# Fused squared-ReLU attention and GELU feed-forward: full-width k transfers, a list-scheduled opening, and the first k by a hardware queue

## The chip, the cores and the metric

The kernel runs on one core of one Trainium2 chip. The metric is device time in microseconds (us) of one execution, and quoted times are medians of several executions. Each execution also has a span, from its first to its last instruction, and a mean granted TensorE clock. The profile is of one execution, so a span can lie a few us off the median time.

Engines are named as in the profile: PE is the matmul engine (TensorE), ACT is ScalarE, DVE is VectorE, POOL is GpSimd, SP is SyncE. SP computes nothing here: it only issues transfers.

## The reference, cut to what matters

```python
# q, k, v: (8 batches, 12 heads, 448 rows, 64)   float32
scores = q @ k.T / sqrt(64)
attn   = maximum(scores, 0) ** 2 / 448
x      = (attn @ v), heads side by side          # (8*448, 768)
out    = gelu(x @ w_in) @ w_out                  # 768 -> 2048 -> 768, float32
```

## The kernel before

Work goes batch by batch, and the parts of a batch are called as follows in this text:

- **Transposes.** q and k are brought into transposed form. Batches 0 to 2 do it on PE, batches 3 to 7 with transfers that transpose, issued by SP ("DMA transposes").
- **Attention.** A quad is four heads. A step is a QK product (L172), a relu on ACT (L180), a square on DVE (L182) and an AV product (L192). DVE then moves the result to `xT`.
- **ffn1** multiplies by `w_in` (L211), and ACT's gelu writes `h_sb`. **ffn2** multiplies by `w_out` (L227); DVE copies the result in two halves into an output tile `osb` (L235), and SP stores the tile.

In the loop over batches, the attention of batch b is woven with ffn1 of b-1 and ffn2 of b-2, so that PE always has something to do.

```python
    opool = pool("opool", 2)          # two output tiles
    f_pp = pool("f_pp", 2, PS)        # two PSUM tiles for ffn1, ffn2 and PE transposes
    ...                               # (cut)
    ROWS = ((KC,) * 4, (128, 128, 128, 64))   # rows of a transpose: q, k
    ...
    def transpose_dma(b):
        for w in (1, 0):
            off = 0
            for t, r in enumerate(ROWS[w]):
                nc.sync.dma_start_transpose(
                    get_T(b)[w][:, :, off : off + r], perm[b][w][:r, t, :]
                )
                off += r
    ...
    def ffn2(pr, t, n):
        if n == 0:
            osbs[pr, t] = opool.tile([128, DM], F32, tag="osb", name="osb")
        ...                           # 16 matmuls into po
        nc.vector.tensor_copy(osb[:, bass.ts(n, ND)], po[:, :ND])
        if n == 1:
            ...
                nc.sync.dma_start(rows[c, p0 : p0 + m, :], osb[j - 128 * t : j - 128 * t + m, :])
    ...
    for b in range(2, B):
        ...
        l = 10 if b == 2 else 2
        prep[l] = nxt                 # permute_k, permute_q, transpose_dma of batch b+1
        ...
        weave(todo, atoms, prep)      # emits work in program order, on all engines
```

Of the kernel before, what the change touches and what calls it, by code (L numbers as in the profile page):

```python
# [8 lines left out]
F32 = mybir.dt.float32  # L9
# [5 lines left out]
NC = S // KC  # L15
KB = 64
NK = S // KB
HP = H // 2
# [9 lines left out]
def kcol(i):  # L28

    return i * 128 if i < 4 else (i - 4) * 128 + 64  # L30
# [3 lines left out]
def kernel(  # L34
# [22 lines left out]
    permpool = pool("perm", 1)  # L57
# [12 lines left out]
    q32 = const.tile([KC, 4, NC * D], F32, tag="q32", name="q32")  # L70

    def load(b, g0, g1):
        h0, h1 = 4 * g0, 4 * g1
        if b not in nq:
            nq[b] = natpool.tile([KC, H, NC * D], BF16, tag="nq", name="nq")
            nk[b] = natpool.tile([128, H, 4 * D], BF16, tag="nk", name="nk")
            vt[b] = vpool.tile([128, G, 2, NK * D], BF16, tag="v", name="v_sb")
        kk = k[b, h0:h1].rearrange("h (p i) d -> p h (i d)", i=NK)
        nc.gpsimd.dma_start(nk[b][:KB, h0:h1, :], kk[:, :, : 4 * D])  # L79
        nc.gpsimd.dma_start(nk[b][KB:, h0:h1, : 3 * D], kk[:, :, 4 * D :])  # L80
        qq = q[b, h0:h1].rearrange("h (p c) d -> p h (c d)", c=NC)
        if b > 0 or g0 > 0:
            nc.gpsimd.dma_start(nq[b][:, h0:h1, :], qq)  # L83
        else:
            nc.sync.dma_start(q32, qq)
        vv = v[b].rearrange("(g j e) (p i) d -> g j p e (i d)", j=2, e=2, i=NK)
        for g in range(g0, g1):
            for j in range(2):
                nc.gpsimd.dma_start(vt[b][64 * j : 64 * j + 64, g], vv[g, j])  # L89
# [4 lines left out]
    def load_win(i):  # L94
        w = moe_w_in.rearrange("(kd p) f -> p kd f", p=128)
        nc.gpsimd.dma_start(win_sb[:, :, bass.ts(i, FF // 4)], w[:, :, bass.ts(i, FF // 4)])
# [6 lines left out]
    qkT, perm = {}, {}  # L103

    def get_T(b):
        if b not in qkT:
            qkT[b] = (
                tpool.tile([128, HP, S], BF16, tag="qT", name="qT"),
                tpool.tile([128, HP, S], BF16, tag="kT", name="kT"),
            )  # L110
        return qkT[b]

    def get_perm(b):
        if b not in perm:
            perm[b] = (
                permpool.tile([KC, NC, DM], BF16, tag="pq", name="pq"),
                permpool.tile([128, 4, DM], BF16, tag="pk", name="pk"),
            )
        return perm[b]


    def permute_q(b, g0=0, g1=G):
        h = slice(4 * g0, 4 * g1)
        pq = get_perm(b)[0].rearrange("p c (h d) -> p h c d", d=D)
        sq = nq[b].rearrange("p h (c d) -> p h c d", d=D)
        nc.vector.tensor_copy(pq[:, h], sq[:, h])  # L126

    def permute_k(b, g0=0, g1=G):
        h = slice(4 * g0, 4 * g1)
        pk = get_perm(b)[1].rearrange("p c (h d) -> p h c d", d=D)  # L130
        sk = nk[b].rearrange("p h (c d) -> p h c d", d=D)
        nc.vector.tensor_copy(pk[:, h, :3], sk[:, h, :3])  # L132
        nc.vector.tensor_copy(pk[:KB, h, 3], sk[:KB, h, 3])  # L133

    ident = const.tile([128, 128], BF16, tag="ident", name="ident")
    ROWS = ((KC,) * 4, (128, 128, 128, 64))

    def transpose_pe(b, g, w, copy):

        tp = f_pp.tile([128, 2, S], BF16, tag="f", name="tp")  # L140
        for j in range(2):
            off = 0
            for t, r in enumerate(ROWS[w]):
                nc.tensor.transpose(  # L144
                    tp[:, j, off : off + r],
                    perm[b][w][:r, t, bass.ts(2 * g + j, 128)],
                    ident[:r, :r],
                )
                off += r
        copy(get_T(b)[w][:, 2 * g : 2 * g + 2, :], tp)  # L150

    def transpose_dma(b):
        for w in (1, 0):
            off = 0
            for t, r in enumerate(ROWS[w]):
                nc.sync.dma_start_transpose(
                    get_T(b)[w][:, :, off : off + r], perm[b][w][:r, t, :]
                )
                off += r
# [4 lines left out]
    xT, hT, asq, pav = {}, {}, {}, {}  # L164

    def qk_step(b, g, i):
        qT, kT = get_T(b)
        ps = s_pp.tile([128, 2, NB], F32, tag="s", name="ps")
        for e in range(2):
            r = slice(64 * e, 64 * e + 64)  # L170
            for j in range(2):
                nc.tensor.matmul(  # L172
                    ps[64 * j : 64 * j + 64, e, :S],
                    kT[r, 2 * g + j, kcol(i) : kcol(i) + KB],
                    qT[r, 2 * g + j, :],
                    start=True,
                    stop=True,
                )
        ar = apool.tile([128, 2, S], BF16, tag="ar", name="a_relu")
        nc.scalar.activation(ar, ps[:, :, :S], AF.Relu, scale=c_att)  # L180
        a2 = apool.tile([128, 2, S], BF16, tag="a2", name="a_sq", bufs=8)
        nc.vector.tensor_mul(a2, ar, ar)  # L182
        asq[b, g, i] = a2

    def av_step(b, g, i):
        if i == 0:
            pav[b, g] = [av_pp.tile([128, NB], F32, tag="av", name="pav") for j in range(2)]
        a2 = asq.pop((b, g, i))
        for j in range(2):
            r = slice(64 * j, 64 * j + 64)  # L190
            for e in range(2):
                nc.tensor.matmul(  # L192
                    pav[b, g][j][64 * e : 64 * e + 64, :S],
                    vt[b][r, g, e, bass.ts(i, D)],
                    a2[r, e, :],
                    start=(i == 0),
                    stop=(i == NK - 1),
                )
        if i == NK - 1:
            if b not in xT:  # L200
                xT[b] = xpool.tile([128, HP, S], BF16, tag="xT", name="xT")
            for j in range(2):
                nc.vector.tensor_copy(xT[b][:, 2 * g + j, :], pav[b, g][j][:, :S])  # L203


    def ffn1(b, m):
        if b // 2 not in hT:
            hT[b // 2] = hpool.tile([128, KF, 2 * S], BF16, tag="h", name="h_sb")
        ph = f_pp.tile([128, NB], F32, tag="f", name="psh")
        for kd in range(KD):  # L210
            nc.tensor.matmul(  # L211
                ph[:, :S],
                win_sb[:, kd, bass.ts(m, 128)],
                xT[b][:, kd, :],
                start=(kd == 0),
                stop=(kd == KD - 1),
            )
        nc.scalar.activation(hT[b // 2][:, m, (b % 2) * S : (b % 2 + 1) * S], ph[:, :S], AF.Gelu)  # L218
# [3 lines left out]
    def ffn2(pr, t, n):  # L222
        if n == 0:
            osbs[pr, t] = opool.tile([128, DM], F32, tag="osb", name="osb")
        po = f_pp.tile([128, NB], F32, tag="f", name="pso")
        for kf in range(KF):
            nc.tensor.matmul(  # L227
                po[:, :ND],
                hT[pr][:, kf, bass.ts(t, 128)],
                wout_sb[:, kf, bass.ts(n, ND)],  # L230
                start=(kf == 0),
                stop=(kf == KF - 1),
            )
        osb = osbs[pr, t]
        nc.vector.tensor_copy(osb[:, bass.ts(n, ND)], po[:, :ND])  # L235
        if n == 1:
            j = 128 * t
            while j < 128 * t + 128:
# [6 lines left out]
                nc.sync.dma_start(rows[c, p0 : p0 + m, :], osb[j - 128 * t : j - 128 * t + m, :])  # L245
                j += m

    def f1(b):
        return [(1.14, ffn1, (b, m)) for m in range(KF)]

    def f2(b):
        tiles = range(0, 3) if b % 2 == 0 else range(3, 7)
        return [(2.6, ffn2, (b // 2, t, n)) for t in tiles for n in range(2)]
# [16 lines left out]
    def run_av(keep):  # L270

        while len(lag) > keep:
            st = lag.pop(0)
            av_step(*st)
            if st[2] == NK - 1:
                break

    def qk(sts):
        for st in sts:
            qk_step(*st)  # L280
            lag.append(st)

    def run(atoms):
        for c, fn, a in atoms:
            fn(*a)

    def steps(b):
        return [(b, g, i) for g in range(G) for i in range(NK)]

    def weave(todo, atoms, prep):  # L290
# [4 lines left out]
        for l in range(0, n, 2):  # L295
            for p in prep.get(l, ()):
                p()
            run_av(0)
            qk(todo[l : l + 2])
            while atoms and done < total * (l + 2) / n - 0.01:  # L300
                done += atoms[0][0]
                run([atoms.pop(0)])
        run(atoms)
# [146 lines left out]
```

## Time and profile before

| | before |
|---|---|
| time, median | 424.91 us (423.57 to 426.17) |
| span of the profiled run | 421.0 us |
| PE busy | 395.6 us, 94% |
| ACT busy | 213.3 us, 51% |
| DVE busy | 186.1 us, 44% |
| POOL busy | 60.9 us, 14% |

PE bounds this kernel: some 25 us of the span are all that it leaves free, of which some 18 lie in the first 75 us. The prediction below shows the views that say so. The chain of work that ended last, as shares of the span by engine ("q" behind an engine's name means its transfer queue):

```profile
PE 87%; DVE 5%; ACT 4%; issue 2%; DMA 1%; POOL 0%; ACTq 0%; DVEq 0%; POOLq 0%
```

### The profile page before, as it was taken

To read this page: it belongs to the slowest core of one execution; us is meant where nothing else is said; L and a number is where in the kernel's file an instruction comes from. 1 tells how busy PE (TensorE), PEld (TensorE's weight loads), DVE (VectorE), ACT (ScalarE), POOL (GpSimd) and SP (SyncE) were. 2 spreads that over 40 slices of the span, in tenths; PEclk is the share of its full clock that TensorE was granted. 3 is DMA by queue.
4 is the path that set the end of the run, shared out by engine and by line. 5 is a ranking of instruction groups with operands and counts; after the bars stand their busy time and mean duration, and the time that the engine had idled before them with its cause. 6 is when DMAs were issued, how large, how long until landed. Compare 5 with 4: busy or idle time off the path is not lost.

```text
span 421.0 us, 7489 instructions
## 1 busy us (share of the span) xinstructions
PE 395.6 (94%) x3152; PEld 200.8 (48%) x3152; DVE 186.1 (44%) x330; ACT 213.3 (51%) x302; POOL 60.9 (14%) x94
## 2 busy tenths in 40 slices
PE   2958998999989999999999999999999999999995
PEld 1323444554545545545445455545455455555562
DVE  1776656336446444464455443463453543300121
ACT  4875665654553556456564565465564654223200
POOL 8363060404104100050005000000000000000000
PEclk9998999999999999999999999999999999999998
DMA  9999399974995990199516990162011111001122
GB/s 141 159 156 200 63 164 209 205 117 78 174 191 85 172 173 15 39 140 166 99 37 92 179 174 2 39 142 66 2 37 39 39 37 29 24 26 37 39 75 75
DMA packets 68417, 41.41 MB, mean 98 GB/s; under 512 B 36640, under 2 KB 64800, under 8 KB 68384
## 3 DMA queue, kind: packets, MB, share of 16 engines
q0 software_dynamic: 35280, 22.58, 38.7%
q1 hardware_dynamic: 33104, 18.36, 22.3%
q8 instruction: 24, 0.39, 0.4%
q14 instruction: 9, 0.07, 0.1%
HBM read 45.61 MB, written 11.01 MB: 135 GB/s over the span
## 4 chain that ended last, share of the span: by engine, by line
PE 87%; DVE 5%; ACT 4%; issue 2%; DMA 1%; POOL 0%; ACTq 0%; DVEq 0%; POOLq 0%
PE pso L227 35%; PE psh L211 34%; PE pav L192 9%; PE ps L172 7%; ACT a_relu L180 4%; PE tp L144 2%; DVE a_sq L182 2%; DMA nk<-in_k_dram 1%; DVE xT L203 1%; DVE qT L150 1%; DVE kT L150 0%; DVE pk L132 0%; DVE pq L126 0%; POOL nk L79 0%; DVE osb L235 0%
## 5 line engine op out<-in xcount | busy, mean ns | idle before, releaser
L180 ACT ACTIVATE a_relu<-ps 128x896 bf16<-128x896 f32 x168 | 144.7, 916 | 116.6 <-PE ps L172 116.6
L211 PE MATMUL psh<-xT,win_sb 128*128 128x448 bf16 x768 | 156.6, 353 | 0.0
L227 PE MATMUL pso<-wout_sb,h_sb 128*128 128x384 bf16 x896 | 152.8, 326 | 0.0
L182 DVE TENSOR_TENSOR a_sq<-a_relu 128x896 bf16<-128x896 bf16 x168 | 104.4, 624 | 91.0 <-ACT a_relu L180 90.6
L227 PEld LDWEIGHTS <-h_sb 128*128 128x128 bf16 x896 | 86.3, 98 | 63.1 <-issue 5.9
L211 PEld LDWEIGHTS <-win_sb 128*128 128x128 bf16 x768 | 70.5, 98 | 79.4 <-issue 19.7
L218 ACT ACTIVATE h_sb<-psh 128x448 bf16<-128x448 f32 x128 | 70.0, 547 | 60.9 <-PE psh L211 60.9
L235 DVE COPY osb<-pso 128x384 f32<-128x384 f32 x56 | 31.2, 558 | 110.3 <-PE pso L227 110.3
L192 PE MATMUL pav<-a_sq,v_sb 64*64 64x448 bf16 x672 | 53.8, 370 | 10.0 <-DVE a_sq L182 5.2
L172 PE MATMUL ps<-qT,kT 64*64 64x448 bf16 x672 | 51.9, 368 | 4.1 <-ACT a_relu L180 2.8
L203 DVE CAST xT<-pav 128x448 bf16<-128x448 f32 x48 | 27.7, 619 | 16.2 <-PE pav L192 16.2
L192 PEld LDWEIGHTS <-v_sb 64*64 64x64 bf16 x672 | 16.3, 107 | 38.7 <-issue 36.9
L79 POOL DMA_DIRECT2D nk<-in_k_dram x12 | 9.4, 783 | 149.8 <-DVE pk L133 139.3
L89 POOL DMA_DIRECT2D v_sb<-in_v_dram x48 | 29.0, 628 | 14.3 <-DMA nk<-in_k_dram 8.9
L172 PEld LDWEIGHTS <-kT 64*64 64x64 bf16 x672 | 21.2, 108 | 20.6 <-issue 9.3
L144 PE MATMUL tp<-ident,pq 112*128 112x112 bf16 x72 | 6.2, 241 | 5.6 <-ACT pq L329 5.6
L83 POOL DMA_DIRECT2D nq<-in_q_dram x11 | 9.5, 859 | 0.7 <-DMA nk<-in_k_dram 0.5
L132 DVE COPY pk<-nk 128x768 bf16<-128x768 bf16 (+1 forms) x14 | 7.1, 510 | 5.4 <-DMA nk<-in_k_dram 5.4
L144 PE MATMUL tp<-ident,pk 128*128 128x128 bf16 x72 | 8.6, 232 | 0.4 <-DVE pk L132 0.4
L80 POOL DMA_DIRECT2D nk<-in_k_dram x12 | 8.4, 703 | 3.5 <-DMA win_sb<-in_moe_w_in_dram 3.5
L144 PEld LDWEIGHTS <-pk 128*128 128x128 bf16 x72 | 5.5, 101 | 5.5 <-DVE a_sq L182 1.2
L144 PEld LDWEIGHTS <-pq 112*128 112x128 bf16 x72 | 4.5, 112 | 7.4 <-ACT pq L329 5.6
(18 smaller groups left out, 32.8 us busy)
## 6 DMA issues: line engine op xcount, KB each, us to landing
v_sb<-in_v_dram POOLq DMA_DIRECT2D x48, 112.0 KB, 13.6
nq<-in_q_dram POOLq DMA_DIRECT2D x6, 672.0 KB, 14.8
win_sb<-in_moe_w_in_dram POOLq DMA_DIRECT2D x4, 768.0 KB, 10.2
wout_sb<-in_moe_w_out_dram POOLq DMA_DIRECT2D x2, 1536.0 KB, 16.9
out_dram<-osb SPq DMA_DIRECT2D x8, 336.0 KB, 2.8
nk<-in_k_dram POOLq DMA_DIRECT2D x6, 384.0 KB, 7.1
out_dram<-osb SPq DMA_DIRECT2D x8, 288.0 KB, 2.6
out_dram<-osb SPq DMA_DIRECT2D x8, 240.0 KB, 2.8
```

What stands on the lines that cost most here:

```text
L83: nc.gpsimd.dma_start(nq[b][:, h0:h1, :], qq)
L89: nc.gpsimd.dma_start(vt[b][64 * j : 64 * j + 64, g], vv[g, j])
L144: nc.tensor.transpose(tp[:, j, off : off + r], perm[b][w][:r, t, bass.ts(2 * g + j, 128)], ident[:r, :r],)
L172: nc.tensor.matmul(ps[64 * j : 64 * j + 64, e, :S], kT[r, 2 * g + j, kcol(i) : kcol(i) + KB], qT[r, 2 * g + j, :], start=True, stop=True,)
L180: nc.scalar.activation(ar, ps[:, :, :S], AF.Relu, scale=c_att)
L182: nc.vector.tensor_mul(a2, ar, ar)
L192: nc.tensor.matmul(pav[b, g][j][64 * e : 64 * e + 64, :S], vt[b][r, g, e, bass.ts(i, D)], a2[r, e, :], start=(i == 0), stop=(i == NK - 1),)
L203: nc.vector.tensor_copy(xT[b][:, 2 * g + j, :], pav[b, g][j][:, :S])
L211: nc.tensor.matmul(ph[:, :S], win_sb[:, kd, bass.ts(m, 128)], xT[b][:, kd, :], start=(kd == 0), stop=(kd == KD - 1),)
L218: nc.scalar.activation(hT[b // 2][:, m, (b % 2) * S : (b % 2 + 1) * S], ph[:, :S], AF.Gelu)
L227: nc.tensor.matmul(po[:, :ND], hT[pr][:, kf, bass.ts(t, 128)], wout_sb[:, kf, bass.ts(n, ND)], start=(kf == 0), stop=(kf == KF - 1),)
L235: nc.vector.tensor_copy(osb[:, bass.ts(n, ND)], po[:, :ND])
```

## The change

Its intent is to shorten the opening, the first 75 us:

1. **Quads regrouped.** k and v are laid out so that one transfer fills 128 partitions. `w_in`'s rows are permuted to match, which takes three transfers per quarter in place of one. A k quad then is seven 128x128 blocks in place of rows of 128, 128, 128 and 64.
2. **A list-scheduled opening.** Operations carry dependencies, buffers and assumed durations. A scheduler picks, at each moment, the one that can start first. Batch 0's attention runs by half sequences, so that ffn1 of batch 0's first half can start early.
3. **First k by a hardware queue** (ACT's), in float32, for POOL's queue. The first q comes by SP's queue in float32, as before, but only half of it comes first.

From batch 2 on, PE's order is given to the scheduler as a fixed list, and so are those of POOL and SP. The core of the diff, much cut:

```diff
+class Scheduler:
+    ...
+    def run(self, fixed):             # fixed: engine -> list whose order is kept
+    ...
-        kk = k[b, h0:h1].rearrange("h (p i) d -> p h (i d)", i=NK)
-        nc.gpsimd.dma_start(nk[b][:KB, h0:h1, :], kk[:, :, : 4 * D])
-        nc.gpsimd.dma_start(nk[b][KB:, h0:h1, : 3 * D], kk[:, :, 4 * D :])
+            nc.gpsimd.dma_start(nk[b][:, 2 * g0 : 2 * g1], kv_view(k, b, g0, g1))
 ...
+    nc.scalar.dma_start(k32, kv_view(k, 0, 0, 1))
+    nc.sync.dma_start(q32, q_view(0, 0, 1, 0, HC))
 ...
+    def add_T_dma(b):
+        for g in range(G):
+            ...
+            op = sch.add((("SP", 0.9, 12.0),), fn, [Pk[b, g]] + old_T(b))
+            sp_q.append(op)
+        for c in range(NC):
+            ...
+            op = sch.add((("SP", 0.9, 12.0),), fn, [Pq[b, g, c] for g in range(G)] + old_T(b))
+            sp_q.append(op)
 ...
+        if n == 1:                    # in add_f2
+            st = sch.add((("SP", 0.3, 2.5),), store, [ev], frees=("osb",))
+            sp_q.append(st)
 ...
     for b in range(2, B):
+        add_steps(steps(b))
+        if b + 1 < B:
+            ...
+            add_T_dma(b + 1)          # appends seven transposes to sp_q
+        ...
         x1, x2 = f1(b - 1), f2(b - 2) # f2 appends its stores to sp_q, after them
 ...
+    sch.run({"PE": pe_q, "POOL": pool_q, "SP": sp_q})
```

## The prediction

> **What bounds the kernel now.** I read the windows view first, cut where the stages change: the first QK matmul starts at 8.93 us, batch 0's last relu ends at about 35.9, and batch 2's interleaved stretch begins with the QK at 75.22. Columns: window, its length, then busy us (instructions) of PE, PEld, DVE, ACT, POOL, then granted clock, DMA share, GB/s.
>
> ```profile
> 0.00:8.93 8.93, 2.19 (x16) 1.37 (x16) 1.43 (x5) 3.44 (x4) 7.83 (x17) 1.00 0.90 140
> 8.93:35.90 26.97, 20.10 (x208) 8.50 (x211) 18.48 (x38) 19.48 (x23) 13.83 (x22) 0.95 1.15 164
> 35.90:75.22 39.32, 34.69 (x329) 16.71 (x324) 25.09 (x51) 25.38 (x36) 10.79 (x15) 0.99 1.01 157
> 75.22:421.00 345.78, 338.66 (x2609) 174.23 (x2608) 141.07 (x237) 165.05 (x239) 28.46 (x43) 1.00 0.52 86
> ```
>
> From 75.22 on PE is busy 98% with ACT and DVE below half: that part is bound by PE's own matmuls, and the part of the 7 us not busy is mostly the last store. The first 75 us hold about 18 us of idle PE. The waits view, for PE before 75.22 and then after it, says on what:
>
> ```profile
> PE tp L144 <- ACT pq L329: 5.6, 1, 5.6
> PE pav L192 <- DVE a_sq L182: 3.3, 5, 2.1
> PE pav L192 <- DVE xT L203: 3.0, 5, 1.7
> PE ps L172 <- ACT a_relu L180: 2.8, 9, 0.6
> PE pav L192 <- DMA win_sb<-in_moe_w_in_dram: 1.8, 1, 1.8
> ```
> ```profile
> PE pav L192 <- DVE a_sq L182: 1.9, 5, 0.4
> ```
>
> So the opening is a chain of first load, cast, transposes, then relu, square and eviction, with PE issuing in a hand-written order. The timeline of ACT shows how fast batch 0's attention can go and how it is broken:
>
> ```profile
> 24.71 5.78 ACT L180 ACTIVATE a_relu<-ps 128x896 bf16<-128x896 f32 x7 [1.57 <-PE ps L172]
> 33.19 0.92 ACT L180 ACTIVATE a_relu<-ps 128x896 bf16<-128x896 f32 x1 [2.70 <-PE ps L172]
> 34.90 0.92 ACT L180 ACTIVATE a_relu<-ps 128x896 bf16<-128x896 f32 x1 [0.79 <-PE ps L172]
> ```
>
> Seven relus in 5.78 us is one per 0.81-0.83 us; 21 of them need 17.2 us, and batch 0 took 27. Between the groups ACT waits for PE, which waits for an eviction or a transpose queued behind something else. The page's slice rows say that DMA is saturated in most of the first 40 us and that the clock drops once:
>
> ```profile
> PEclk9998999999999999999999999999999999999998
> DMA  9999399974995990199516990162011111001122
> ```
>
> **What the Trainium skill says.** "DMA: Bandwidth & Descriptors", Rules for kernel authors, advises one 128-partition transfer instead of two to disjoint halves, and its section SWDGE vs HWDGE vs iDMA says that a cast during the transfer needs the GpSimd queue. The trace agrees with the second as far as it goes: the one load on SP (q) lands in float32 and is cast by ACT in 1.045 us. "TensorE: Matmul & The Clock Gate", Part 1, says PE starts at half clock and falls back after about 3.4 us of idleness. Agreed: four QK matmuls show 0.59 us up to 18 us and 0.38 after, and 0.59 again near 34-36 after the idle stretch at 29-32. "TensorEngine Tiling (Array Packing)", Key Properties, says that a change of tiling mode drains PE. Agreed: 12 ffn1 matmuls after attention take 2.38 us, 18 with none before 3.40, so a switch costs 2.38 - 12 x 0.189 = 0.11 us. "ScalarE: Activation LUTs", What ACT_TABLE_LOAD costs, gives 186 ns + 0.833 N, with 93 ns of overlap back to back: 932 for N = 896, the trace has 916; 559 for 448, the trace has 547. From it I estimate 0.28-0.37 us for the new 224-column activations.
>
> **The change part by part.** Everything from batch 2 on keeps its PE order, as the comparison of instruction orders shows (same runs of QK, AV, ffn1, ffn2). So the span is 345.8 us plus the moment at which batch 2's stretch starts (75.2 now), and what that moment gains comes off the measured 424.9.
>
> (1) First loads. k comes by ACT's queue, half of q by SP's: 0.46 + 0.23 MB of float32. Now 0.46 MB of q lands at 4.5 and k through POOL at 6.3. At the 380 GB/s which the DMA rows show around 2.5-3.5 us, 0.69 MB takes 1.8 us; begun at 1.8 and with about 0.8 to completion, both are there at 4.4. The casts (ACT 512 elements, about 1.1 us in two pieces; DVE 896 float32 elements, about 1.0) end at 5.5. Half of q means four transposes for eight. The cold transposes and kT's copy (0.62) put the first QK at 7.7 for 8.93: -1.2 us.
>
> (2) K transposes. Rows of 128, 128, 128, 64 become seven full 128x128 per quad. Now they cost
>
> ```profile
> 54.37 0.87 PE L144 MATMUL tp<-ident,pk 128*128 128x128 bf16 x8
> 55.17 0.57 PE L144 MATMUL tp<-ident,pq 112*128 112x112 bf16 x8
> 55.67 0.57 PE L192 MATMUL pav<-a_sq,v_sb 64*64 64x448 bf16 x8
> ```
>
> 0.80 us from start to start for k, 0.50 for q of equal count: the two 64-row ones change the tiling mode and cost the extra 0.3-0.4. Ten quads up to 75 us, two later: -4 us of PE work, -0.8 of it certain (batch 2's last two quads); the rest counts only where PE is the bound.
>
> (3) Batch 0's attention by half sequences, in pairs: 20 full relus and 2 half ones for 21. ACT: 20 x 0.81 + 2 x 0.45 = 17.1, two qT copies of 448 (0.9), four xT copies of 224 (1.2): 19.2 us. First relu about 8.3, so 27.5, plus some 2 us of stalls while PE is cold (cold QK and AV pairs are 0.37 each, 0.75 of each 0.81 slot, and two quads of transposes do not fit beside them): 29.5 for 35.9.
>
> (4) Batch 1 with ffn1 of batch 0 in halves. ACT: 21 x 0.81 = 17.0, 17 half gelus by 0.35 = 6.0, copies 2.4: 25.4, giving 55 for the last relu. Then square and AV, about 1.2, of which part is covered, 66 half ffn1 matmuls at an estimated 0.10 (6.6), transposes and their two copies (2.2): batch 2's stretch begins at about 65.
>
> (5) PE as a check. Transposes 10 x (0.39 + 0.39 + 0.2 for switches) = 9.8; batch 0's 84 half steps at 0.11 = 9.2 (0.095 by columns, more for four weight loads, which take 0.11-0.13); batch 1's 42 steps at 0.19 = 8.0; 32 half ffn1 at 0.60 = 19.2; about 40 further switches by 0.1 = 4; cold clock about 5; start 5.5: 60.7 us. PE and ACT are thus both close to full, and neither order can be perfect: I put 65.5, so -9.7, and -0.8 from (2): 424.9 - 10.5 = 414.4.
>
> (6) Loads. Batch 0, batch 1 and w_in are the same 14.5 MB of float32 as now; the k pieces of 512 and 384 bytes become 896, w_in's grow in number from 4 issues to 12. At 340-400 GB/s (170-200 of the bf16 that the DMA rows count) all are in by 40-43 us; batch 1's third quad is wanted at about 45. Batch 2 and w_out follow without the present gap at 45-52 us.
>
> **Rivals.** (a) DMA stays the bound: the DMA row is at 9 for most of the first 40 us and nothing fewer is loaded. Against: much of that is the loader running ahead, and only 1.8 us of PE's waits name a DMA. If it holds, batch 1's last quad slips by 3-4 us and the time is 418. (b) PE becomes the bound in the opening: twice the number of attention matmuls and ffn1 matmuls with the same weight loads for half the columns, more switches, a cold clock. For: my sum has only 5 us to spare. If a half step costs 0.19 as the full one does, 84 x 0.08 = 6.7 us more: 419-421. (c) The static order, fixed from assumed durations on all engines, is wrong where the chip differs, and the strict order on ACT and DVE turns a late load into waits after 75 us too, where now there are 2: +2-4 us. (d) Better than thought: the denser opening warms the clock at about 14 us for 19 and keeps it (now 3.4 us are lost half again at 33-36), and ACT runs unbroken: batch 2 begins at 61, time 410.
>
> **Range and chances.** The PE sum makes about 409.5 the floor; (a) or (b) alone give 418-421. So 410 to 420 for eight in ten. The 2% line is 416.4, inside the range and above the centre by 2: faster 0.62, same 0.35, slower 0.03 (only if (b) and (c) add up).
>
> **What would show it.** In the new profile: first QK at 7.7 +- 0.5; batch 0's relus ending at 28-31; batch 2's first QK pair at 63-68 and from there to the end 345 +- 1.5; PE idle before that at 9-12 us for 18, of which about 5 at the start; k transposes at 0.4 per quad; no clock drop at 33-36. Wrong if the tail after batch 2's start grows, if PE's waits name k, q or w_in loads for over 2 us, or if half steps take near 0.19.

## More of the kernel before

`weave` emits everything in program order: an engine gets its instructions in the order in which the code reaches them. `transpose_dma(b+1)` stands inside the weave, after the first steps of batch b, and so it comes into SP's queue between the stores of output tiles.

SP's timeline in batch 2's stretch; columns: start, duration in us, queue, line, kind of transfer, destination<-source, number.

```profile
97.31 0.81 SPq L245 DMA_DIRECT2D out_dram<-osb  x2
100.39 6.04 SPq L156 DMA_TRANSPOSE kT<-pk  x4
106.48 12.85 SPq L156 DMA_TRANSPOSE qT<-pq  x4
119.43 12.35 SPq L245 DMA_DIRECT2D out_dram<-osb  x6
```

SP issues the first finished tile (two stores, since its rows lie in two strips of the output), and only then the eight DMA transposes. These occupy it for 6.04 + 12.85 = 18.9 us. Then come the stores of the next tiles.

## The result, and the profile after

| | before | changed |
|---|---|---|
| time, median | 424.58 us (423.57 to 426.17) | 440.41 us (439.93 to 440.92) |
| span of the profiled run | 421.0 us | 438.2 us |
| start of batch 2's stretch | 75.22 us | 64.16 us |
| from there to the end | 345.78 us | 374.04 us |
| PE busy | 395.6 us, 94% | 397.0 us, 91% |

The changed kernel is slower: the ratio is 1.037 (95% interval 1.033 to 1.041). Ratios here are the mean time of one kernel's fast runs over that of the other's of the same rounds, so not quite the ratio of the medians quoted. (The before column has one more run than the section above.)

The windows view of the changed kernel, cut as in the prediction: first QK, near the end of batch 0's last relu (which ends at 30.66, a little before the cut), batch 2's stretch. Columns as there.

```profile
0.00:8.17 8.17, 1.30 (x13) 1.04 (x13) 1.82 (x6) 2.20 (x4) 7.04 (x14) 1.00 0.84 170
8.17:32.00 23.83, 21.50 (x430) 15.66 (x431) 20.79 (x53) 21.80 (x35) 13.66 (x21) 1.00 1.33 199
32.00:64.16 32.16, 29.65 (x362) 21.34 (x362) 20.46 (x45) 26.74 (x51) 7.46 (x9) 1.00 1.17 189
64.16:438.20 374.04, 344.59 (x2606) 175.61 (x2605) 132.70 (x249) 171.84 (x256) 10.35 (x12) 0.97 0.48 78
```

The opening did what it was made for: 11.1 us gained (75.22 - 64.16). The last line lost 28.3 us (374.04 - 345.78) with the same PE work in it: 2606 recorded matmuls against 2609. The net is 17.2 us of span. Of the 28.3, 5.9 are longer PE busy time (344.59 - 338.66) at a mean clock of 0.97; the rest is idle PE. The slice rows and the chain of the changed kernel's page show where:

```profile
PE   3899899995489789999999949999999999999995
PEclk9999999999599979999999969999999999999999
DMA  9999999189519911399117961173011110111122
...
PE 70%; DMA 9%; SPq 9%; DVE 4%; ACT 3%; POOL 2%; issue 2%; DVEq 0%; POOLq 0%; ACTq 0%
```

A slice is 10.96 us. PE has three holes, at slices 10 to 11, 14 and 24 (counted from 1, roughly 99 to 121, 142 to 153 and 252 to 263 us), and the clock falls in or after each. SP's queue, absent from the chain before, now holds 9% of the span, and transfers 9% for 1%; 3% of the span are output stores, while 5% is the load of `w_in` in the opening. The waits view of the changed kernel, PE before 64.16 and then PE and DVE after it (who waited <- on what: us in total, times, longest):

```profile
PE tp L377 <- ACT pq L324: 6.2, 1, 6.2
PE ps L433 <- ACT a_relu L443: 1.3, 4, 0.4
...
DVE osb L244 <- DMA out_dram<-osb: 30.5, 3, 12.9
PE psh L531 <- DVE osb L244: 11.7, 2, 7.0
PE pso L565 <- DVE osb L244: 10.1, 1, 10.1
```

The first two lines answer the five of the prediction: of the waits inside the opening only the first, for the first q, is left in size. The last three have no line to answer to in the kernel before. DVE, about to copy into an output tile, waits three times for that tile's store; PE waits three times for DVE, 21.8 us in all. SP's timeline of the changed kernel at the first hole says why the store was late:

```profile
89.17 6.08 SPq L398 DMA_TRANSPOSE kT<-pk  x3
95.36 13.44 SPq L407 DMA_TRANSPOSE qT<-pq  x4
108.84 12.12 SPq L587 DMA_DIRECT2D out_dram<-osb  x6
```

All seven transposes now come before the first store of the stretch. The first tile was finished before 90 us, but its store was issued at 108.84, when SP was through with 19.5 us of transposes. DVE's and PE's timelines show the first tile's last copy and what followed (in brackets: idle before, and its releaser):

```profile
85.64 0.56 DVE L244 COPY osb<-pso 128x384 f32<-128x384 f32 x1 [1.63 <-PE pso L565]
...
114.47 0.56 DVE L244 COPY osb<-pso 128x384 f32<-128x384 f32 x1 [12.94 <-DMA out_dram<-osb]
115.08 4.47 PE L565 MATMUL pso<-wout_sb,h_sb 128*128 128x384 bf16 x16 [10.08 <-DVE osb L244]
```

There are two output tiles, so the third tile's first copy must wait until the first has been stored. It was wanted at 101.53 (114.47 - 12.94). While DVE waits, PE's two PSUM tiles for ffn stay full, and PE stops for 10.08 us. The same 16 matmuls take 2.77 us elsewhere in this trace and 4.47 here. The Trainium skill, "TensorE: Matmul & The Clock Gate", Part 1, says that the clock halves after some 3.4 us of idleness; after idle times of 10.08, 4.63 and 7.04 us this trace agrees.

The batches that pass without a stall fit this too. In batches 2, 3 and 5 the third tile of the stretch was wanted at 101.53, 147.07 and 247.63, and the held-back stores were issued only at 108.84, 150.65 and 251.93. In batches 4 and 6 it was wanted at 209.64 and 312.33, when the stores had been issued at 205.47 and 295.60.

### The profile page after: what moved, and what is told of

Its sections match the earlier page's. It is cut to its first block, busy times and chain, and to the rows that moved or that the text cites. A ratio compares the mean times of both kernels' runs of the same rounds, so it can differ in the third digit from the quotient of the medians.

```text
span 438.2 us, 7991 instructions
## 1 busy us (share of the span) xinstructions
PE 397.0 (91%) x3407; PEld 213.7 (49%) x3407; DVE 175.8 (40%) x351; ACT 222.6 (51%) x344; POOL 38.5 (9%) x54
## 4 chain that ended last, share of the span: by engine, by line
PE 70%; DMA 9%; SPq 9%; DVE 4%; ACT 3%; POOL 2%; issue 2%; DVEq 0%; POOLq 0%; ACTq 0%
PE pso L565 31%; PE psh L531 27%; SPq L407 8%; PE pav L479 6%; DMA win_sb<-in_moe_w_in_dram 5%; PE ps L433 4%; DMA out_dram<-osb 3%; ACT a_relu L443 3%; DMA nk<-in_k_dram 2%; DVE a_sq L450 2%; DVE osb L244 1%; ACT h_sb L543 1%; SPq L587 1%; POOL nq L199 1%; POOL v_sb L292 1%
## 5 line engine op out<-in xcount | busy, mean ns | idle before, releaser
L443 ACT ACTIVATE a_relu<-ps 128x896 bf16<-128x896 f32 (+1 forms) x169 | 145.6, 918 | 108.0 <-PE ps L433 107.9
L531 PE MATMUL psh<-xT,win_sb 128*128 128x448 bf16 (+1 forms) x864 | 162.1, 338 | 11.7 <-DVE osb L244 11.7
L450 DVE TENSOR_TENSOR a_sq<-a_relu 128x896 bf16<-128x896 bf16 (+1 forms) x169 | 104.0, 621 | 92.0 <-ACT a_relu L443 91.6
L543 ACT ACTIVATE h_sb<-psh 128x448 bf16<-128x448 f32 (+1 forms) x144 | 72.5, 510 | 72.8 <-PE psh L531 72.6
L479 PE MATMUL pav<-a_sq,v_sb 64*64 64x448 bf16 (+1 forms) x756 | 54.3, 342 | 3.5 <-DVE a_sq L450 3.2
L433 PE MATMUL ps<-qT,kT 64*64 64x448 bf16 (+1 forms) x756 | 51.3, 338 | 3.1 <-ACT a_relu L443 1.3
L244 DVE CAST xT<-pav 128x448 bf16<-128x448 f32 (+1 forms) x30 | 16.6, 561 | 15.9 <-PE pav L479 15.9
L246 ACT CAST xT<-pav 128x448 bf16<-128x448 f32 (+1 forms) x24 | 12.1, 505 | 5.1 <-PE pav L479 5.1
L324 DVE COPY pq<-nq 112x512 bf16<-112x512 bf16 (+1 forms) x52 | 11.8, 279 | 0.2 <-DMA nq<-in_q_dram 0.2
L292 POOL DMA_DIRECT2D v_sb<-in_v_dram x12 | 9.4, 779 | 1.6 <-DMA nk<-in_k_dram 0.8
```

The source lines that it names most:

```text
L244: V.tensor_copy(dst, src)
L246: A.copy(dst, src)
L292: nc.gpsimd.dma_start(vt[b][:, 2 * g0 : 2 * g1], kv_view(v, b, g0, g1))
L433: nc.tensor.matmul(ps[64 * j : 64 * j + 64, e, x * w : x * w + w], kT[r, g, i * 128 + 64 * j : i * 128 + 64 * j + 64], qT[r, 2 * g + j, co ...
L443: A.activation(box["ar"][:, :, :used], box["ps"][:, :, :used], AF.Relu, scale=c_att)
L450: V.tensor_mul(box["a2"][:, :, :used], ar, ar)
```

## The experiments

**Theory 1**: the tail was lost because SP's order puts each batch's transposes ahead of the first finished tile's store, while there are only two output tiles. **Rivals**: the stores themselves became slow; or the fixed orders on ACT and DVE, or the denser opening and its loads, are what hurts the tail. Ten kernels were run, all gave correct results. Their times are compared with runs of the kernel before in the same rounds (medians 424.12 to 424.39).

### Store ahead of the transposes

Only SP's list of the changed kernel is reordered:

```diff
+            n0 = len(sp_q)
             add_T_dma(b + 1)
+            n1 = len(sp_q)
 ...
         x1, x2 = f1(b - 1), f2(b - 2)
+        if b + 1 < B:
+            sp_q[n0:] = sp_q[n1 : n1 + 1] + sp_q[n0:n1] + sp_q[n1 + 1 :]
```

> The changed kernel with one change of order on the SP queue: in each batch the store of the first finished output tile is issued before the seven DMA transposes, as in the kernel before; nothing else is moved. Theory 1 (stores queued behind transposes hold both output buffers, so DVE, then PE, stand still three times): the three stalls go, the stretch from batch 2's first QK takes about 346 us as before (374 in the changed kernel), the time is 411 to 415 us, and no wait of DVE on an output transfer is over 1 us. Rival A (the regrouped k, with its 128x7x128 transposes, or the busier DMA, makes the later stretch slow by itself): 430 to 440. Rival B (the fixed order on ACT and DVE is what costs after 75 us): also over 425.

Measured: 412.64 us (412.47 to 413.39), ratio 0.972 (0.968 to 0.976). Its windows, cut at batch 2's stretch, and its SP timeline:

```profile
0.00:63.22 63.22, 52.04 (x802) 38.12 (x802) 42.91 (x102) 50.70 (x88) 28.23 (x42) 1.00 1.20 193
63.22:410.90 347.68, 338.62 (x2606) 173.97 (x2605) 133.13 (x249) 171.80 (x256) 10.34 (x12) 1.00 0.50 84
...
85.28 0.81 SPq L587 DMA_DIRECT2D out_dram<-osb  x2
88.23 5.88 SPq L398 DMA_TRANSPOSE kT<-pk  x3
```

The tail is 347.68 us instead of 374.04, its PE busy time is back at the kernel before's (338.62 against 338.66), and the clock no longer drops. One store moved per batch gives back 27.8 us. The opening is as short as before (63.22). Theory 1 is confirmed from this side. The rival orders on ACT and DVE can be checked in the traces: by operation, tile names and shapes, the instructions of PE, ACT, DVE and POOL come in the same order here as in the changed kernel, all 344 of ACT and 351 of DVE. So those orders did not change, and the loss went. The tail is still 1.9 us longer than 345.78. PE's waits name 1.4 us for a transfer of `qT` that the kernel before does not have; the kernel with three output tiles, further below, has no such wait and a tail of 346.45 us.

### The same fault put into the kernel before

The kernel before keeps everything, but its stores are held until the transposes have been issued:

```diff
         if n == 1:
+            def store():
+                put(pr, t, osb)
+            held.append(store)
+            if sent[0]:
+                flush()
 ...
-            nxt = [later(permute_k, b + 1), later(permute_q, b + 1), later(transpose_dma, b + 1)]
+            nxt = [later(permute_k, b + 1), later(permute_q, b + 1), later(transpose_dma, b + 1), sent_T]
```

> The kernel before with only its SP queue reordered to that of the changed kernel: the store of the batch's first finished output tile is held back until the eight DMA transposes have been issued. Theory 1: it slows by as much as the changed kernel lost after its opening, 20 to 30 us, so 445 to 455, with waits of DVE on output transfers and a TensorE clock that drops in the same places. Rivals A and B: the order alone costs under 5 us, so 425 to 430.

Measured: 457.65 us (455.76 to 460.85), ratio 1.078 (1.072 to 1.084). Its waits:

```profile
DVE osb L235 <- DMA out_dram<-osb: 38.3, 4, 12.5
...
PE psh L211 <- DVE osb L235: 15.0, 3, 6.9
...
PE pso L227 <- DVE osb L235: 9.4, 1, 9.4
```

The same three kinds of wait appear in a kernel that has none of the change: four stalls instead of three, 33 us lost, a little more than expected. (In the profiled run, the slowest of the four, batch 2's stretch begins at 79.17 us for 75.22, so some 4 us of its loss lie before the stalls; its tail alone is 33.9 us longer.) So nothing in the new opening is needed for the loss.

### A third output tile

SP's order stays as the change made it:

```diff
-    opool = pool("opool", 2)
+    opool = pool("opool", 3)
-    sch = Scheduler({"s": 2, "ar": 3, "a2": 8, "av": 2, "f": 2, "osb": 2})
+    sch = Scheduler({"s": 2, "ar": 3, "a2": 8, "av": 2, "f": 2, "osb": 3})
```

> The changed kernel, SP order untouched, with three output buffers for two ([...]the list scheduler is told of three). Theory 1: a third buffer lets the three tiles of an even batch wait for their stores without stopping DVE, and shortens the stall of odd batches; about 20 of the 28 us come back, so 416 to 424. Rivals A and B: no effect, 438 to 441.

Measured: 411.94 us (411.71 to 411.95), ratio 0.970 (0.967 to 0.973), below the expected range. Its SP timeline:

```profile
88.76 6.36 SPq L398 DMA_TRANSPOSE kT<-pk  x3
95.22 13.32 SPq L407 DMA_TRANSPOSE qT<-pq  x4
108.59 3.45 SPq L587 DMA_DIRECT2D out_dram<-osb  x6
```

The stores are as late as in the changed kernel (108.59 against 108.84), and no wait of DVE for a store is left. PE, ACT, DVE and POOL again have their instructions in the same order as the changed kernel. So a late store by itself costs nothing; it costs only when the tile is wanted. I had expected the third tile to hide part of the delay; it hid all of it.

### Both together, and the third tile in the faulty kernel before

> Store first and three output buffers together. Theory 1: nothing is left for the third buffer to do, so within 1 us of the store-first kernel, 411 to 415. If it is faster by over 2 us, store first alone leaves a stall that the theory has not named.

Both mends in one kernel: 412.04 us (411.16 to 412.51), ratio 0.970 (0.967 to 0.973). The two do not add, as they should not if they mend the same thing.

> The kernel before with its transposes first on SP (the order that cost it 33 us with two output buffers) and a third output buffer. If the loss needs both, the stores late and only two buffers, it goes: 423 to 428 us, and no wait of DVE on an output transfer over 1 us. If the late stores cost by another way too (late qT, DMA contention), 432 or more stays.

The kernel before with its stores held back, and three tiles: 424.10 us in the median, ratio 1.000 (0.997 to 1.003). All 33 us are back. One of its four runs, the profiled one, took 589.35 us at a mean clock of 0.66; it is left out of the ratio, and its trace is not used, so the expected absence of DVE's waits was not checked. This run and the one with transposes first and two tiles together show that the loss needs both parts: transposes first, and only two tiles.

### Stores issued by ACT

If SP's order is the trouble, stores might leave SP altogether:

```diff
-                nc.sync.dma_start(
+                nc.scalar.dma_start(
 ...
-            st = sch.add((("SP", 0.3, 2.5),), store, [ev], frees=("osb",))
-            sp_q.append(st)
+            sch.add((("ACT", 0.1, 2.5),), store, [ev], frees=("osb",))
```

> The changed kernel with its output stores issued from ACT's queue; SP keeps the transposes, in the same places, and two output buffers stay. If the stores were late because SP issues in order and stood in its transposes (theory 1), they now leave as soon as their tile is copied: 411 to 415 us, no long wait of DVE on an output transfer. If they were late because the transfers themselves are slow beside the DMA transposes (rival C: the DMA rings are busy), the stores still land late, the stalls stay in part, and the time is over 425.

Measured: 434.13 us (430.9 to 436.27), ratio 1.023 (1.018 to 1.029), unclear against the 2% line; it is better than the changed kernel and far from what I expected. Its waits, among others:

```profile
PE pav L479 <- DVE a_sq L450: 11.6, 20, 2.4
...
PE ps L433 <- DMA qT<-pq: 5.2, 1, 5.2
```

No DVE wait for a store is left, so that much of theory 1 holds. But ACT takes its instructions in order too, and now has stores between its relus. The Trainium skill, "DMA: Bandwidth & Descriptors", section Anatomy of one DMA (which is written of GpSimd's transfers), says that a semaphore wait of a transfer happens on the issuing sequencer. ACT's timeline agrees: two stores are issued at 127.39, when DVE's copy of their tile has ended at 127.36, and the relu behind them begins at 128.68, when they are through. Another two stores hold ACT from 137.47 for 3.31 us; the relu behind them begins at 140.88, and PE's AV then waits 2.41 us for its square.

The tail is 21.2 us longer than with three tiles on SP (367.65 against 346.45). PE's account of it is 8.9 us more of waiting for squares (11.0 against 2.1), 5.2 us for the transfer of batch 3's `qT`, 1.0 us for gelus, and 6.3 us of longer busy time at a mean clock of 0.98; these make the sum but for 0.2 us. Batch 3's q transposes occupied SP for 17.2 us instead of 13.4.

As for the rival that stores are slow: the median from issue to landing is 2.7 us in both kernels, but the longest is 5.2 us in the changed one and 10.4 us here, and the q transposes have a median of 12.6 us here for 9.9. In the three holes of the changed kernel DVE goes on 5.6, 4.0 and 5.7 us after the stores' issue. So stores beside transposes are slow at times, which can make up some 7 of DVE's 30.5 us of waits; the rest is late issue. No experiment separates the two further.

### SP's operations list-scheduled

The lists of PE and POOL stay fixed, SP's is dropped, and a transpose is modelled with 2.8 us of SP's time (the 19.5 us of seven, divided) instead of 0.9:

```diff
-            op = sch.add((("SP", 0.9, 12.0),), fn, [Pk[b, g]] + old_T(b))
-            sp_q.append(op)
+            op = sch.add((("SP", 2.8, 12.0),), fn, [Pk[b, g]] + old_T(b))
 ...                                   # the same for q; stores: no sp_q either
-    sch.run({"PE": pe_q, "POOL": pool_q, "SP": sp_q})
+    sch.run({"PE": pe_q, "POOL": pool_q, })
```

> The changed kernel with the SP queue given to the list scheduler like ACT and DVE, instead of the order in which the program creates its operations, and the SP time of a transpose told as 2.8 us (the trace of the changed kernel has 6.1 for three and 13.4 for four) for 0.9. The order that comes out puts a store before the transposes in batches 2, 3 and 5, where the changed kernel stalled, and leaves them behind in 4 and 6, where it did not. Theory 1: 411 to 415, no stall. If the stalls move to batches 4 or 6, 418 to 428.

Measured: 412.45 us (411.87 to 412.75), ratio 0.974 (0.971 to 0.977), no stall. The scheduler does find a good order on SP, once it is allowed to and knows what a transpose costs there. Which of the two it needed was not tried.

### What the parts of the opening are worth

Three kernels start from the one with the store moved ahead (412.64 us, ratio 0.9721) and take one part each out of it. They ran on another chip than it, so ratios to the kernel before are compared, not times. A difference of ratios times 424.3 us gives us; its uncertainty, from the two intervals, is about 2 us.

First q and k of batch 0 through POOL's queue. This undoes more than the change did, since in the kernel before the first q already came by SP:

```diff
-    nc.scalar.dma_start(k32, kv_view(k, 0, 0, 1))
-    nc.sync.dma_start(q32, q_view(0, 0, 1, 0, HC))
 ...
+    add_q(0, 0, 1, 0, HC)
+    add_k(0, 0, 1)
```

> The store-first kernel with the first quad's q and k loaded by the GpSimd queue (cast to bf16 on the way) instead of the SP and ACT hardware queues. By the prediction's step 1 the hardware queues are worth about 1.2 us: first QK at 9 to 9.5 us for 8.2, time 413.5 to 415. If the later opening has slack (PE or ACT catch up), under 0.5 us.

Measured: 414.76 us (414.23 to 416.49), ratio 0.978 (0.975 to 0.981), unclear against the 2% line. So the hardware queues for both are worth (0.9782 - 0.9721) x 424.3 = 2.6 us. The first QK comes at 9.36 instead of 8.34 us, and batch 2's stretch begins at 66.49 instead of 63.22. What the k queue alone is worth, which is the part that the change made, was not measured.

Two 64-row transposes added to each k quad that PE transposes. Their result is never read; they stand for the tiling-mode changes that the old layout had:

```diff
+                if i in (3, 6):
+                    nc.tensor.transpose(tp[:, 896:960], pk[:64, g, 0:128], ident[:64, :64])
```

> The store-first kernel with two 64-row transposes put back into each quad of k that PE transposes (into unused columns, so the result is unchanged), which restores the changes of tiling mode of the kernel before. Step 2 says 0.3 to 0.4 us more for each of 12 quads, 4 us if PE is the bound all the way: 416 to 417. If ACT is the bound in the opening, only the three quads of batch 2 and a few others count: 413 to 414.5.

Measured: 414.18 us (413.18 to 414.35), ratio 0.976 (0.973 to 0.978): 1.5 us more, which is within its uncertainty of none. In the trace a k quad takes 0.85 to 0.87 us with them, once the clock is up, and 0.40 without. (The 12 quads of the expectation are nine in the trace.) The cost on PE is a little over the 0.3 to 0.4 predicted, but little of it reaches the end.

Batch 0 by whole sequences (first q load, transposes, steps and ffn1 whole; the scheduler finds its own order for them):

```diff
-    st0 = halves(0)
+    st0 = steps(0)
 ...
-        add_f1(0, m, 0, bias=BIAS)
+        add_f1(0, m, bias=BIAS)
```

> The store-first kernel with batch 0's attention over whole sequences instead of halves (all of q loaded for each quad first, ffn1 of batch 0 in whole tiles), the scheduler told so. If the halves matter (less data needed before ffn1 of batch 0 can fill PE), the second QK quads wait for loads and ffn1 starts later: +3 to +6, so 415 to 419. If the gain of the opening is only in the list-scheduled order, within 1 us: 412 to 413.5.

Measured: 417.60 us (417.28 to 417.68), ratio 0.984 (0.981 to 0.987), within 2% of the kernel before. The halves, with the smaller first q load that comes with them (first QK at 10.02 instead of 8.34 us), are worth (0.9841 - 0.9721) x 424.3 = 5.1 us, by its value the largest part. Of the 11.8 us that the mended kernel gains (0.0279 x 424.3), these three account for 9.2 if they add, and the first of them holds more than the change made. What list-scheduling and wide loads are worth was not measured apart. The traces give the same order of size: batch 2's stretch begins at 63.22 to 64.16 us in the six kernels that have the whole opening, and at 65.52, 66.49 and 68.77 without full transposes, hardware queues and halves.

## Why the prediction was wrong

The prediction said 414.4 us, with 410 to 420 as the range; the changed kernel took 440.41. Point by point:

- **What bounds the kernel, and the opening: right.** Batch 2's stretch was predicted at about 65 and began at 64.16. PE's idle time before it was predicted at 9 to 12 us, and is 64.16 - 52.45 = 11.7 (52.45 is the sum of PE's first three windows).
- **Part (1), first loads: right in kind, too large.** The first QK came at 8.17 us, not at 7.7: ACT's cast of q began at 5.38, so the load took longer than the estimate (landed at about 5.3, not 4.4), while the casts took less (ACT 0.71 us, DVE 0.63). Gained: 0.8 us instead of 1.2.
- **Part (2), k transposes: the duration is right, the count wrong, the worth not told apart from the 0.8 us called certain (the experiment gave 1.5, within about 2).** The prediction counts ten quads before 75 us and two later; its trace has seven and two (56 and 16 transposes of `pk`, eight per quad). The changed kernel's PE timeline has 0.40 us from the start of a k quad to the next work:

```profile
31.97 0.56 PE L359 MATMUL tp<-ident,pk 128*128 128x128 bf16 x7
32.37 0.74 PE L531 MATMUL psh<-xT,win_sb 128*128 128x224 bf16 x6
```

- **Part (3), halves on ACT: right, a little late.** Batch 0's last relus are in this part of ACT's timeline of the changed kernel, and end at 30.66, not 29.5, inside the 28 to 31 given as a sign:

```profile
16.87 4.97 ACT L443 ACTIVATE a_relu<-ps 128x896 bf16<-128x896 f32 x6 [0.30 <-PE ps L433]
29.31 1.35 ACT L443 ACTIVATE a_relu<-ps 128x896 bf16<-128x896 f32 x2
```

  Six relus in 4.97 us are 0.83 each, as before. But the scheduler had put gelus of batch 0's own first half between the last ones: work of the next part, done early.
- **Parts (4) to (6), PE sum and loads: near.** The sum gives PE 55.2 us of work before batch 2's stretch (60.7 less the start of 5.5), and it was 52.45; the three quads counted too many, at 0.98 us each, are 2.9 of that. Half ffn1 matmuls took the estimated 0.10 us each, half attention steps 0.095 to 0.10 instead of 0.11. No wait of PE before 64.16 names a load among those of over 0.2 us. The clock no longer drops at 33 to 36 us, as rival (d) said. The prediction reads the old drop there as agreeing with a fall after 3.4 us of idleness, but PE's longest idle time between 14 us and that drop is 1.80 us, so this trace does not show it. The holes of the changed kernel, of 4.63 us and more, are what agrees.
- **The step that failed** stands at the head of the change part by part: "Everything from batch 2 on keeps its PE order, as the comparison of instruction orders shows (same runs of QK, AV, ffn1, ffn2). So the span is 345.8 us plus the moment at which batch 2's stretch starts". The first sentence is true, and the second does not follow from it. PE's time depends also on the orders of the engines that free its buffers. SP's order had changed, as the diff shows (`add_T_dma` appends to `sp_q` before `f2`) and the two SP timelines: a q load, two stores and then transposes before; a q load, seven transposes and then stores after. The prediction compares PE's order only; SP was not on the chain of the kernel before. What the runs put in the step's place is a tail of 374.04 us: three stalls, 21.8 us of PE's waiting and 5.9 us of half-clock matmuls.
- **Rival (c) was near it.** It had a static order going wrong in the tail, but on ACT and DVE through a late load, and at 2 to 4 us. The order that failed was SP's, through a late store, and it cost 28.3.
- **The test that the prediction named worked.** "Wrong if the tail after batch 2's start grows" is what happened, and the windows view showed it at once.

With the order on SP mended the prediction's sum comes near: 412.64, 411.94 and 412.45 us against 414.4. Part of that is luck. As a span the prediction says 410.5 (65.5 + 345.0), and 410.1 to 410.9 were measured, but the stretch begins 2 us earlier than predicted and its tail is 1.4 to 2.7 us longer, and these cancel. The 414.4 itself takes the gain off a median of 424.91 us, while its windows are those of a run of 422.99 us. The cause is shown from both sides: taking either part of it away restores the time, and adding it to the kernel before takes 33 us.

The mended versions beat both kernels. The change with three output tiles takes 411.94 us, 3.0% less than the kernel before, and with the store moved ahead 412.64 us, 2.8% less.

## What to carry to other kernels

When a rewrite keeps the order of the engine that bounds the kernel, compare the other queues too, above all those that only issue transfers: an in-order queue that seems idle decides when buffers come free. Before a long transfer is put ahead of a short one there, ask which buffer the short one frees, how many of it there are, and when the next is wanted. In a list scheduler, an order given as fixed is not repaired by the scheduler, and its durations should come from a trace: here a transpose was assumed to take 0.9 us of SP and took 2.0 (k) to 3.4 (q).

## What the Trainium skill lacked or had wrong

- **"DMA: Bandwidth & Descriptors", DMA Transpose (X-bar)**, gives no time for which a transpose holds the queue that issues it. Here three k transposes held SP for 6.08 us and four q transposes for 13.44, while stores waited behind them; six stores held it for 3.45 us where the tiles were ready.
- **The same page, Issuing engines are not separate DMA queues**, calls the sequencer's time for initiating a transfer "usually small relative to the DMA itself". A q transpose held SP for 3.4 us here (13.44 for four), beside a median of 9.9 us from issue to landing. The page does not say what may stand behind it: in the changed kernel that order cost 28.3 us of span, and moving the stores to ACT's sequencer brought little of it back (434.13 us against 411.94 for the best).
- **"TensorEngine Tiling (Array Packing)", Key Properties**, says that a change of tiling mode drains PE, without a figure. Two 64-row transposes among seven 128-row ones cost 0.45 to 0.47 us per quad here (0.85 to 0.87 against 0.40), the two instructions themselves included.
